# Low bits of converted weights from ScalarE into PSUM, and PSUM banks of their own for scores and for weighted sums in the first batch

## The chip, the core and the metric

The kernel runs on one core of a Trainium2 chip. A core has five engines that each take a list of instructions in order: PE (TensorE, matrix products), ACT (ScalarE), DVE (VectorE), POOL (GpSimd) and SP (SyncE, which here only issues DMAs). They work on SBUF; PE writes to PSUM, which has eight banks of 512 fp32 words in each of 128 partitions. An instruction waits on semaphores that other engines raise. The metric is device time in microseconds (us) for one execution.

## What is computed

Attention over a narrow window and over block summaries, then two mixing layers. Cut to what matters (B=4, H=8, S=768, D=64, blocks of 32, window 16, d_model 512, d_tok 256, d_ch 1536):

```python
k_sum = k.reshape(B, H, 24, 32, D).max(axis=3)
v_sum = v.reshape(B, H, 24, 32, D).mean(axis=3)
scores = concat([where(|i - j| < 16, scale * q @ k.T, -1e9), scale * q @ k_sum.T + log(32)])
a = exp(scores - max); a = a / (sum(a) + 1e-9)
x = (a @ concat([v, v_sum])).transpose -> (B, S, H * D)
h = maximum(x.T @ w_tok1, 0) @ w_tok2          # token mixing, over S
u = x + h.T
out = u + maximum(u @ w_ch1, 0) @ w_ch2        # channel mixing, over 512 -> 1536 -> 512
```

The four weights arrive as 64-bit floats, which the kernel sees as pairs of 32-bit words.

## The kernel before

**Work.** The batches are worked on one after the other. A batch has four pairs of heads; a pair has two groups of three tiles of queries. For head n and group g the names are `sc_n_g` (scores, PE, into PSUM), `e_p_g` (masked scores, DVE, then their exponentials and the row sums `den`, ACT), `et_n_g` (transposed, PE, into PSUM), `eT_n_g` (copied to SBUF, ACT) and `av_n` (weighted sum of v, PE); DVE multiplies it by `rec`, one over the row sum, into `x`. Before that DVE takes the block maxima `ks` of k, PE the block means `vm_p` of v for a pair, ACT copies them to `vs_b_p` and POOL spreads them into the rows of v that hold the summaries. Token mixing is `t1p_b_p` (PE), `t1_b_p` (its rectified high half on ACT, the low half on DVE), `up_b_half_p` (PE) and `u_b_half_p`. Channel mixing goes through the 1536 hidden columns in steps f: `hp` (24 matmuls for two steps), `h` (high half on ACT, low half on DVE) and `acc`, the sum over f.

The first batch has nothing to overlap with: its attention and token mixing run alone, and channel mixing begins when they are done. In later batches attention and token mixing are put between the steps f of the batch before.

**Conversion of weights.** Every fp32 product is made of three products of parts (high with high, high with low, low with high), so each weight is turned into two parts. `w_tick(i)` converts 512 columns of 64-bit words in SBUF. Ticks 0 to 2 make the weights of `t1p` (`wt1`), 3 to 5 those of `up` (`wt2`), and 6 to 29 in turn those of `hp` (`w1_f`) and `acc` (`w2_f`), the last of them during the first batch's channel mixing. A tick has these steps:

- ACT `absolute` (L1426): the upper word without its sign, as a float
- `clamp` (L1430): into the range of fp32, on POOL, for ticks 0 to 2 on DVE
- DVE `shift` (L1435): up three bits and masked; written to a PSUM bank `wp_i` in ticks 10 to 23, to SBUF in the others
- DVE `sign` (L1442): with the sign of the upper word
- DVE `low` (L1449): with the top three bits of the lower word
- ACT high part (L1472, twice) and POOL low part (L1478, twice), not in ticks 0 to 2

So three DVE operations are done for every tick.

**Order.** `Plan` collects every piece of work with its engine, an assumed duration, a rank and the keys that it reads and writes, plays a list schedule with assumed costs (250 GB/s for loads among them) and writes a fixed list for each engine from it. What an engine does next is never decided on the chip. Keys are pairs of a tile and a part; the framework that the lists are written in adds the semaphore waits, and it goes by tiles. Loads go through SP's list in order; eight semaphores are used in turn, so a load also waits for the eighth before it.

**Banks.** In PSUM the tag `att` has two banks, `mm` two, and `acc0` to `acc3` one each. In the first batch (`state["phase"] == "start"`) scores, transposes and weighted sums take `att, att, acc0, acc1` in turn; `vm_p` takes `acc2`, a tile for each p; `t1p` and `up` take `mm, mm, acc3` in turn. `TICKS` says after which step s of the attention how many ticks have been asked for.

Of the kernel before, what the change touches and what calls it, by code (L numbers as in the profile page):

```python
# [190 lines left out]
def tile_attention_mixer(  # L191
# [135 lines left out]

    def first_means(p):

        pt = bank(f"vm_{p}", ["acc2"])  # L330
# [5 lines left out]
        def sums():  # L336
            for t in range(NT):
                for j in range(2):
                    nc.tensor.matmul(
                        pt.t[at[j] : at[j] + NB, :D],  # L340
# [353 lines left out]
    def tok1(b, p):  # L694
        x2, a = x_t[b, p]
        pt = bank(f"t1p_{b}_{p}", ["mm", "mm", "acc3"])

        def products():
# [10 lines left out]
            writes=[(pt, 0)], rank=R_ATT,  # L709
# [1 line left out]
        split_t1(
            b, p, lambda: pt.t[:, :DTOK].rearrange("p (k c) -> p k c", k=2), (pt, 0), 0.39
# [666 lines left out]
    def w_tick(i, behind=()):  # L1379
# [31 lines left out]
        if psum:  # L1411
            pb = bank(f"wp_{i}", ["att"])
            between, bkey = (lambda: pb.t.bitcast(I32)), (pb, 0)
        else:
            between, bkey = mid, parts[0]
# [8 lines left out]
        def absolute():  # L1424
            for j, cs in enumerate(pieces):
                nc.scalar.activation(mid()[:, cs].bitcast(F32), words(j, 1).bitcast(F32), AF.Abs)  # L1426
# [19 lines left out]

        def low():
            for j, cs in enumerate(pieces):
                nc.vector.scalar_tensor_tensor(  # L1449
                    out=mid()[:, cs], in0=words(j, 0), scalar=29, in1=between()[:, cs],  # L1450
                    op0=ALU.logical_shift_right, op1=ALU.bitwise_or,
                )

        stt = 0.7 if room else 0.85
        add("act", 0.68 if room else 0.85, absolute, reads=keys, writes=parts, rank=rank)
        if first:
            add("dve", 0.45, lambda: clamp(nc.vector), writes=parts, rank=rank)
        else:
            add("pool", 0.75, lambda: clamp(nc.gpsimd), writes=parts, rank=rank)
        add("dve", 0.6 if psum else 0.5, shift, reads=parts, writes=[bkey], rank=rank)  # L1460
        add("dve", stt, sign, reads=keys, writes=[bkey], rank=rank)
        add("dve", stt, low, reads=keys + [bkey], writes=parts, rank=rank)
# [204 lines left out]
```

## Time and profile before

| | |
|---|---|
| median of 3 runs | 571.74 us (571.09 to 572.02) |
| the profiled execution | 569.56 us |
| its span in the profile | 567.6 us |
| granted TensorE clock | 1.00 throughout |
| PE, DVE, ACT, POOL busy | 552.1, 355.6, 258.2, 258.9 us |
| data moved by DMA | 99.52 MB |

The span runs from the first to the last instruction that the profiler records, so the 2.0 us between 569.56 and 567.6 lie outside it. Times inside the profile count from the span's start. An engine that is busy for 97% of the span sets the end wherever it is dense; what the others do counts only where this engine waits for them, so the places to look at are its gaps. A duration in the timeline reaches into the next instruction where the engine is pipelined; the distance between two starts is then the cost.

### The profile page before, as it was taken

Reading aid. Unit: us, or ns where it says so; the run is one execution under the profiler, and the core shown is the slowest. Engines: PE = TensorE matmul, PEld = TensorE weight load, DVE = VectorE, ACT = ScalarE, POOL = GpSimd, SP = SyncE. Lnnn points to the kernel's source line nnn. Section 1 sums busy time; section 2 is a strip of 40 time slices with the busy share of each in tenths; the row PEclk is TensorE's granted clock in tenths of the full one; section 3 lists DMA queues with packets and bytes.
Section 4 is the critical chain, followed back from the end, with each engine's and each line's share of the span. In section 5 each row is a group of like instructions: output and inputs, shape, how many; then the busy total and the mean of one; then the engine's idle time right before and its main releaser. Section 6 shows DMA issues by size and latency. Waiting matters only on the chain.

```text
span 567.6 us, 12757 instructions
## 1 busy us (share of the span) xinstructions
PE 552.1 (97%) x4629; PEld 485.3 (85%) x4629; DVE 355.6 (63%) x982; ACT 258.2 (45%) x789; POOL 258.9 (46%) x325
## 2 busy tenths in 40 slices
PE   7789999999999999999999999999999999999997
PEld 4588888868989988777799997787789999999997
DVE  4698899997474246455563335445352484899984
ACT  4677675437385334232242314242233452567642
POOL 0236586753032510157797511048879711444111
PEclk9999999999999999999999999999999999999999
DMA  8953558653656017758795606677779663643621
GB/s 267 345 169 124 193 191 274 214 179 127 203 157 194 25 39 197 189 182 208 245 261 146 139 13 189 145 189 193 192 182 313 170 263 102 203 131 97 205 92 64
DMA packets 133774, 99.52 MB, mean 175 GB/s; under 512 B 88272, under 2 KB 112464, under 8 KB 133712
## 3 DMA queue, kind: packets, MB, share of 16 engines
q1 hardware_dynamic: 133568, 98.52, 58.2%
q8 instruction: 36, 0.59, 0.4%
q14 instruction: 26, 0.21, 0.1%
q10 hardware_dynamic: 144, 0.20, 0.1%
HBM read 68.60 MB, written 28.31 MB: 171 GB/s over the span
## 4 chain that ended last, share of the span: by engine, by line
PE 76%; DVE 11%; DMA 6%; ACT 3%; issue 2%; POOL 1%; SPq 1%; ACTq 0%; DVEq 0%
PE acc L896 21%; PE hp L853 20%; PE t1q L748 5%; PE up L792 4%; PE av L558 4%; PE pb L1126 3%; PE qb L1126 3%; PE sc L427 3%; DMA w<-in_w_ch 3%; PE qa L1126 2%; PE pc L1126 2%; PE pa L1126 2%; PE qc L1126 2%; DVE wb L1449 2%; ACT e L451 1%
## 5 line engine op out<-in xcount | busy, mean ns | idle before, releaser
L896 PE MATMUL acc<-h,w 128*128 128x512 f32 (+1 forms) x864 | 165.4, 341 | 1.4 <-DVE h L870 1.4
L853 PE MATMUL hp<-u,w 128*128 128x512 f32 (+1 forms) x864 | 163.6, 339 | 0.0
L896 PEld LDWEIGHTS acc<-h,w 128*128 128x128 f32 x864 | 133.4, 189 | 21.9 <-DVE h L870 1.8
L853 PEld LDWEIGHTS hp<-u,w 128*128 128x128 f32 x864 | 133.3, 188 | 20.2 <-issue 1.3
L451 ACT ACTIVATE e<-e,den 128x120 f32<-128x120 f32 x192 | 73.3, 385 | 55.1 <-DVE den L441 39.0
L870 DVE SCALAR_TENSOR_TENSOR h<-hp,h 128x512 fp32r<-128x512 f32 (+1 forms) x72 | 39.7, 552 | 83.8 <-ACT h L865 83.6
L865 ACT ACTIVATE h<-hp 128x512 fp32r<-128x512 f32 (+1 forms) x72 | 35.1, 488 | 114.4 <-PE hp L853 113.3
L973 POOL TENSOR_TENSOR s<-s,w 128x256 f32<-128x256 f32 x84 | 61.7, 741 | 5.0
L441 DVE CUSTOM_DVE_ANT_0 e<-sc,mask_sb 128x120 f32<-128x120 f32 x192 | 41.4, 277 | 13.0 <-PE sc L427 10.8
L1478 POOL TENSOR_TENSOR w<-wb,w 128x256 fp32r<-128x256 f32 x48 | 37.7, 805 | 19.0 <-ACT w L1472 18.8
L935 POOL TENSOR_TENSOR ot<-ot,u 128x512 f32<-128x512 f32 (+1 forms) x24 | 23.8, 1019 | 43.4 <-DVE ot L927 42.6
L792 PE MATMUL up<-wt,t 128*128 128x512 f32 (+2 forms) x192 | 39.0, 343 | 0.0
L451 ACT ACTIVATION_READ_ACCUMULATOR e<-e,den 128x1 f32 x192 | 36.2, 189 | 0.0
L734 POOL TENSOR_TENSOR xs<-x,xs 128x512 fp32r<-128x512 f32 x18 | 23.6, 1310 | 25.5 <-DMA v<-vs 17.9
L410 POOL MEMSET e<- 128x48 f32 x16 | 2.2, 138 | 67.8 <-DMA away<-e 32.7
L792 PEld LDWEIGHTS up<-wt,t 128*128 128x128 f32 x192 | 30.3, 189 | 2.6
L427 PE MATMUL sc<-k,q 64*64 64x120 f32 x768 | 28.1, 271 | 1.9 <-PE et L489 0.7
L427 PEld LDWEIGHTS sc<-k,q 64*64 64x64 f32 x768 | 20.5, 132 | 10.9 <-issue 7.0
L558 PEld LDWEIGHTS av<-v,eT 120*64 120x64 f32 x768 | 24.1, 138 | 6.7 <-issue 4.5
L558 PE MATMUL av<-v,eT 120*64 120x64 f32 x768 | 26.7, 224 | 2.7 <-issue 1.1
L1472 ACT ACTIVATE w<-wb 128x256 fp32r<-128x256 f32 x48 | 18.1, 413 | 23.0 <-DVE wb L1449 22.8
L748 PE MATMUL t1q<-xs,ws 128*128 128x256 f32 x216 | 28.5, 283 | 0.0
(128 smaller groups left out, 862.1 us busy)
## 6 DMA issues: line engine op xcount, KB each, us to landing
w<-in_w_ch SPq DMA_DIRECT2D x48, 256.0 KB
k<-in_kw SPq DMA_DIRECT2D x16, 720.0 KB
v<-in_vw SPq DMA_DIRECT2D x32, 288.0 KB
q<-in_q SPq DMA_DIRECT2D x16, 384.0 KB
away<-e SPq DMA_DIRECT2D x16, 384.0 KB
eT<-away SPq DMA_DIRECT2D x64, 96.0 KB
sums<-s SPq DMA_DIRECT2D x24, 256.0 KB
w2d<-w SPq DMA_DIRECT2D x12, 512.0 KB
```

The costliest lines, as they stand in the source:

```text
L427: nc.tensor.matmul(tiles[j].t[c * QT : (c + 1) * QT, i * NC : (i + 1) * NC], lhsT=qt.t[rows, t * QT : (t + 1) * QT], rhs=kt.t[rows, t, :], ...
L441: nc.vector.tensor_tensor_reduce(out=e.t[:, j, i * P : i * P + NC], in0=tiles[j].t[:, i * NC : (i + 1) * NC], in1=mask_sb[:, mv, :], op0=A ...
L451: nc.scalar.activation(ei, ei, AF.Exp, bias=den_t[n].t[:, 1, T : T + 1], scale=-1.0, accum_out=den_t[n].t[:, 0, T : T + 1],)
L558: nc.tensor.matmul(pv[cs, T], lhsT=eT[:NC, T % (TT // 2), cs], rhs=v.t[:NC, 2 * T + c], start=True, stop=True,)
L748: nc.tensor.matmul(pt.t[:, 2 * P * k : 2 * P * (k + 1)], lhsT=ws[:, wp, T, ks], rhs=xs[:, xp, T], start=(c == 0 and k == 0 and T == 0 and ...
L792: nc.tensor.matmul(pt.t[:, :nt], lhsT=t1.t[:, part, ks], rhs=wt2[w].t[:, k, h0 : h0 + nt], start=(far and k == 0 and i == 0), stop=(k == D ...
L853: nc.tensor.matmul(pt.t[:, :nt], lhsT=w1_t[f].t[:, w, c], rhs=us[c].t[:, part], start=(i == 0), stop=(i == len(ops) - 1),)
L870: lambda: nc.vector.scalar_tensor_tensor(out=h.t[:, 1], in0=pt.t[:, :nt], scalar=0.0, in1=h.t[:, 0].bitcast(F32), op0=ALU.max, op1=ALU.sub ...
L896: nc.tensor.matmul(slot.t[:, c0 : c0 + nt], lhsT=w2_t[f].t[:, w, o * P : (o + 1) * P], rhs=h.t[:, part], start=(f == 0 and w == 0 and part ...
L973: nc.gpsimd.tensor_tensor(out=out_, in0=left, in1=right, op=op)
L1126: nc.tensor.matmul(bank_.t[:, :HS], lhsT=w(i), rhs=x(j), start=first and n == 0, stop=True, skip_group_check=True,)
L1478: lambda hi=hi, lo=lo, source=source: nc.gpsimd.tensor_tensor(out=lo(), in0=source(), in1=hi().bitcast(F32), op=ALU.subtract),
```

## The change

**Conversion.** `absolute` now scales the upper word by 2^-80, with the clamp's bounds scaled alike. A new ACT step `last_bits` reads the lower word as an unsigned integer and writes its top three bits as an integer into a PSUM bank. `shift` becomes one DVE operation that shifts the clamped word and ors it with these bits, in PSUM; `sign` ands the result with the upper word's sign and writes it to SBUF. `low` is gone. The clamp is on POOL for all ticks. All 30 ticks use a PSUM bank: `acc3` for ticks 0 to 5, `acc0` and `acc1` in turn for 6 to 9, `att` from 10 on. Ticks 3 to 5 get the rank of attention, and tick 6 is asked for later (the entry `12: 7` is gone).

**Banks of the first batch.** Scores alone rotate over `att, att, acc0, acc1`. Transposes and weighted sums take `mm, mm`. All `vm_p` and all `t1p` share one tile, `vm_bank` on `acc2`: `t1p` its first 256 columns, `vm_p` 64 columns each behind them. `up` of the first two pairs take `acc3`, of the last two `acc0, acc1, att, att`.

**Plan.** Loads before 25 us are costed at 360 GB/s.

```diff
-    RATE, LAND = 250.0, 2.2
+    RATE, FIRST, LAND = 250.0, 360.0, 2.2
...
         "start": ["att", "att", "acc0", "acc1"],
+        "turned": ["mm", "mm"],
...
+    def att_bank(name, turned=False):
+        start = state["phase"] == "start"
+        return bank(name, BANKS["turned" if turned and start else state["phase"]])
+
+    def tok_bank(name, late):
+        if state["phase"] == "start":
+            return bank(name, ["acc0", "acc1", "att", "att"] if late else ["acc3"])
         return bank(name, BANKS[state["phase"]])
...
+    vm_bank = plan.slot(ps, [P, 512], F32, "acc2", "vm", 1)
...
-        pt = bank(f"vm_{p}", ["acc2"])
+        pt, cs = vm_bank, slice(DTOK + D * p, DTOK + D * (p + 1))
...
-            pt = att_bank(f"et_{n}_{g}")
+            pt = att_bank(f"et_{n}_{g}", True)
...
-            pt, v, den = att_bank(f"av_{n}"), v_t[n], den_t[n]
+            pt, v, den = att_bank(f"av_{n}", True), v_t[n], den_t[n]
...
-        pt = bank(f"t1p_{b}_{p}", ["mm", "mm", "acc3"])
+        pt = vm_bank
...
-        first, rank = two[0][2] is None, R_ATT if i < TOKT else R_W
-        psum = 10 <= i < 24
+        first, rank = two[0][2] is None, R_ATT if i < 6 else R_W
...
+        pb = bank(f"wp_{i}", ["acc3"] if i < 6 else ["acc0", "acc1"] if i < 10 else ["att"])
+        bits = lambda: pb.t.bitcast(I32)
...
+        def last_bits():
+            for j, cs in enumerate(pieces):
+                nc.scalar.activation(
+                    bits()[:, cs], words(j, 0).bitcast(U32), AF.Copy, bias=LOW_BIAS,
+                    scale=LOW_SCALE,
+                )
...
         def shift():
-            nc.vector.tensor_scalar(
-                out=between(), in0=mid(), scalar1=3, scalar2=0x3FFFFFFF,
-                op0=ALU.logical_shift_left, op1=ALU.bitwise_and,
+            nc.vector.scalar_tensor_tensor(
+                out=bits(), in0=mid(), scalar=3, in1=bits(),
+                op0=ALU.logical_shift_left, op1=ALU.bitwise_or,
             )
 
         def sign():
             for j, cs in enumerate(pieces):
                 nc.vector.scalar_tensor_tensor(
-                    out=between()[:, cs], in0=words(j, 1), scalar=-0x40000000,
-                    in1=between()[:, cs], op0=ALU.bitwise_and, op1=ALU.bitwise_or,
+                    out=mid()[:, cs], in0=words(j, 1), scalar=0x7FFFFFFF, in1=bits()[:, cs],
+                    op0=ALU.bitwise_or, op1=ALU.bitwise_and,
                 )
 
-        def low():
-            for j, cs in enumerate(pieces):
-                nc.vector.scalar_tensor_tensor(
-                    out=mid()[:, cs], in0=words(j, 0), scalar=29, in1=between()[:, cs],
-                    op0=ALU.logical_shift_right, op1=ALU.bitwise_or,
-                )
...
-    TICKS = {3: 3, 8: 6, 12: 7, 17: 9, 19: 10}
+    TICKS = {3: 3, 8: 6, 17: 9, 19: 10}
```

The lists come out of the plan anew. Three places of them matter below. On SP, among the first batch's loads, the token weights of tick 2 were followed by these before (the number behind a name is that of its buffer):

```order
L269 DMA v_4_338<-in_vw 96x768
L269 DMA v_5_357<-in_vw 96x768
L269 DMA k_3_364<-in_kw 128x1440
L269 DMA q_3_366<-in_q 128x768
L1396 DMA w_3_368<-in_w_tok2 128x512 x2
```

In the changed kernel k_3 and q_3 come first at the same place:

```order
L280 DMA k_3_282<-in_kw 128x1440
L280 DMA q_3_284<-in_q 128x768
L280 DMA v_4_364<-in_vw 96x768
L280 DMA v_5_384<-in_vw 96x768
L1406 DMA w_3_387<-in_w_tok2 128x512 x2
```

So v of the third pair of heads has moved behind k and q of the fourth; the two blocks have the same bytes together.

On ACT, in the first batch, this stood before around the copy `t1_0_1` of the second `t1p` (L682) and the copy `vs_0_3` of the last block means (L359; e_2_1 is finished ahead of the piece):

```order
L682 ACTIVATE t1_0_1_629<-t1p_0_1_584 128x256
L1472 ACTIVATE wt2_0_632<-wb_3_573 128x256 x2
L451 ACTIVATE e_3_0_638,den_6_639<-e_3_0_638,den_6_639 128x120
L500 ACTIVATE eT_4_1_654<-et_4_1_634 120x384
L500 ACTIVATE eT_5_1_659<-et_5_1_642 120x384
```

In the changed kernel the same part of ACT's list reads (L695 is the copy `t1`, L372 `vs`, L1432 `absolute`, L1438 `last_bits`, L1477 the high part, L464 the exponential):

```order
L695 ACTIVATE t1_0_0_668<-vm_200 128x256
L1438 ACTIVATE wp_4_670<-w_4_435 128x512
L464 ACTIVATE e_2_1_532,den_4_398<-e_2_1_532,den_4_398 128x120
L372 ACTIVATE vs_0_3_688<-vm_200 24x64 x2
L1432 ACTIVATE wb_5_693<-w_5_474 128x512
L464 ACTIVATE e_2_1_532,den_5_405<-e_2_1_532,den_5_405 128x120
L1477 ACTIVATE wt2_0_637<-wb_4_628 128x256 x2
L1438 ACTIVATE wp_5_700<-w_5_474 128x512
L695 ACTIVATE t1_0_1_703<-vm_200 128x256
L464 ACTIVATE e_2_1_532,den_4_398<-e_2_1_532,den_4_398 128x120
L464 ACTIVATE e_2_1_532,den_5_405<-e_2_1_532,den_5_405 128x120
L464 ACTIVATE e_3_0_574,den_6_575<-e_3_0_574,den_6_575 128x120
```

`vs_0_3`, which stood behind eT_5_1 and the first two exponentials of e_3_1, has moved ahead of four exponentials of e_2_1, and the tile that it reads, `vm`, is also the one that `t1p` is written to.

On PE, behind the block means of the last pair, the changed kernel has (the first row is t1p_0_1):

```order
L714 MATMUL vm_200<-x_0_0_362,wt1_367 128x128 x12
L502 MATMUL et_4_1_710<-identf_66,e_2_1_532 120x128 x3
L502 MATMUL et_5_1_716<-identf_66,e_2_1_532 120x128 x3
L571 MATMUL av_4_731<-v_4_364,eT_4_0_609 64x64 x6
L571 MATMUL av_4_731<-v_4_364,eT_4_1_721 64x64 x6
L571 MATMUL av_5_746<-v_5_384,eT_5_0_625 64x64 x6
L571 MATMUL av_5_746<-v_5_384,eT_5_1_729 64x64 x6
L502 MATMUL et_6_0_772<-identf_66,e_3_0_574 120x128 x3
L502 MATMUL et_7_0_777<-identf_66,e_3_0_574 120x128 x3
```

Before, t1p_0_1 stood ahead of the scores of the last pair and those ahead of et_4_1; the block means of the last pair came only behind av_5 and the pair's second scores. Now they stand ahead of t1p_0_1, and et_4_1 follows it at once.

More of the change, by code (lines that the diff above doesn't have):

```diff
@@ L14 @@
 I32 = mybir.dt.int32
+U32 = mybir.dt.uint32
 AF = mybir.ActivationFunctionType
@@ L41 @@
 HALF = NF // 2
-HI_MAX = 122879.9921875
+HI_SCALE = 2.0**-80
+HI_MIN, HI_MAX = 2.0**-95, 122879.9921875 * HI_SCALE
+LOW_SCALE = 2.0**-29 * (1 - 2.0**-20)
+LOW_BIAS = 7.5 * 2.0**-20 - 0.5
 NU = B * H
@@ L151, in _order @@
                 if w.kb:
-                    dma = max(dma, now) + w.kb / self.RATE
+                    dma = max(dma, now) + w.kb / (self.RATE if now > 25 else self.FIRST)
                     w.end = dma + self.LAND
@@ L351, in first_means @@
         add(
-            "pe", 1.6, sums, reads=[(v_t[2 * p], 0), (v_t[2 * p + 1], 0)], writes=[(pt, 0)],
+            "pe", 1.6, sums, reads=[(v_t[2 * p], 0), (v_t[2 * p + 1], 0)], writes=[(pt, p)],
             rank=R_H,
@@ L359, in first_means @@
                 lambda j=j: nc.scalar.activation(
-                    s.t[WIN:NC, j * D : (j + 1) * D], pt.t[at[j] : at[j] + NB, :D], AF.Copy
+                    s.t[WIN:NC, j * D : (j + 1) * D], pt.t[at[j] : at[j] + NB, cs], AF.Copy
                 ),
-                reads=[(pt, 0)], writes=[(s, j)], rank=R_EVAC,
+                reads=[(pt, p)], writes=[(s, j)], rank=R_EVAC,
             )
@@ L708, in tok1 @@
             "pe", 2.8, products, reads=x_keys(b, p) + [(wt1, i) for i in range(3)],
[L709 removed]
+            writes=[(pt, "t")], rank=R_ATT,
         )
         split_t1(
[L712 removed]
+            b, p, lambda: pt.t[:, :DTOK].rearrange("p (k c) -> p k c", k=2), (pt, "t"), 0.39
         )
@@ L769, in tok2 @@
         h0, nt = H0[b][half], HT[b][half]
-        pt = bank(
-            f"up_{b}_{half}_{p}",
-            ["mm", "mm", "acc3"] if state["phase"] == "start" else BANKS[state["phase"]],
-        )
+        pt = tok_bank(f"up_{b}_{half}_{p}", p >= NP - 2)
         tag, bufs, whole = f"u{half}", 4, b == B - 1
@@ L1410, in w_tick @@
             mid = lambda: wb.t
[L1411 to L1415, printed above, removed]
+        pb = bank(f"wp_{i}", ["acc3"] if i < 6 else ["acc0", "acc1"] if i < 10 else ["att"])
+        bits = lambda: pb.t.bitcast(I32)
         n = 512 if room else 256
@@ L1442, in sign @@
                 nc.vector.scalar_tensor_tensor(
-                    out=between()[:, cs], in0=words(j, 1), scalar=-0x40000000,
-                    in1=between()[:, cs], op0=ALU.bitwise_and, op1=ALU.bitwise_or,
-                )
-        def low():
-            for j, cs in enumerate(pieces):
-                nc.vector.scalar_tensor_tensor(
-                    out=mid()[:, cs], in0=words(j, 0), scalar=29, in1=between()[:, cs],
-                    op0=ALU.logical_shift_right, op1=ALU.bitwise_or,
[L1452 to L1462, printed above, removed]
+                    out=mid()[:, cs], in0=words(j, 1), scalar=0x7FFFFFFF, in1=bits()[:, cs],
+                    op0=ALU.bitwise_or, op1=ALU.bitwise_and,
+                )
+        spent = 0.66 if room else 0.85
+        add("act", spent, absolute, reads=keys, writes=parts, rank=rank)
+        add("pool", 0.75, clamp, writes=parts, rank=rank)
+        add("act", spent, last_bits, reads=keys, writes=[(pb, 0)], rank=rank)
+        add("dve", 0.7, shift, reads=parts, writes=[(pb, 0)], rank=rank)
+        add("dve", 0.7 if room else 0.85, sign, reads=[*keys, (pb, 0)], writes=parts, rank=rank)
         for j in range(0 if first else 2):
@@ L1516, in tile_attention_mixer @@
                 tok2(0, 0, p - 1)
-    while tick < 10:
+    while tick < TICKS[19]:
         w_tick(tick)
```

13 lines of the change are left out of this document (7 added, 6 removed).

## The prediction

> **What bounds the kernel now.** I read the page first, for the engine that ends the span.
>
> ```profile
> PE 552.1 (97%) x4629; PEld 485.3 (85%) x4629; DVE 355.6 (63%) x982; ACT 258.2 (45%) x789; POOL 258.9 (46%) x325
> PE 76%; DVE 11%; DMA 6%; ACT 3%; issue 2%; POOL 1%; SPq 1%; ACTq 0%; DVEq 0%
> ```
>
> PE is busy 97% of the span and carries 76% of the chain that ended last, so a conversion that costs VectorE less is worth only what PE now waits for. The windows view says where PE waits (start:end, length, then busy time and count of PE, PEld, DVE, ACT, POOL, the granted clock, the DMA share, GB/s).
>
> ```profile
> 8.00:29.70 21.70, 16.32 (x357) 12.49 (x349) 14.57 (x69) 14.98 (x63) 3.19 (x4) 1.00 1.01 323
> 29.70:65.50 35.80, 33.35 (x435) 30.31 (x433) 32.08 (x105) 26.95 (x93) 18.22 (x24) 1.00 0.45 144
> 65.50:115.90 50.40, 50.40 (x218) 40.64 (x217) 46.75 (x79) 29.59 (x70) 37.66 (x54) 1.00 0.71 227
> 115.90:118.00 2.10, 0.70 (x4) 0.25 (x2) 2.10 (x6) 1.01 (x3) 1.29 (x3) 1.00 0.61 240
> 118.00:160.00 42.00, 41.65 (x445) 35.63 (x445) 30.32 (x111) 20.42 (x82) 10.78 (x12) 1.00 0.48 156
> 160.00:540.00 380.00, 378.96 (x3020) 340.24 (x3021) 210.33 (x583) 154.00 (x460) 182.19 (x220) 1.00 0.60 170
> 540.00:567.60 27.60, 23.89 (x134) 22.96 (x133) 17.54 (x31) 9.97 (x19) 4.86 (x4) 1.00 0.21 75
> ```
>
> PE's idle time by row is 5.4 us, 2.4, 0, 1.4, 0.35, 1.0 and 3.7. The stretch to 65.5 is the first batch's attention and token mixing, and at 65.53 the first channel-mixing matmul (`hp`) starts. From there the work is the same in both kernels and PE is dense apart from one hole. So only two things count: **when the first `hp` starts**, and **the 1.40 us hole** at 116. PE's timeline has both (start, duration, line, tiles, count, idle time before and its releaser):
>
> ```profile
> 28.23 1.53 PE L339 MATMUL vm<-v,means 96*24 96x64 f32 x48
> 29.69 2.94 PE L701 MATMUL t1p<-x,wt 128*128 128x128 f32 x24
> 35.59 0.92 PE L489 MATMUL et<-identf,e 128*120 128x128 f32 x6 [1.40 <-ACT e L451]
> 41.26 1.62 PE L558 MATMUL av<-v,eT 120*64 120x64 f32 x48 [0.50 <-DVE den L441]
> 50.23 1.27 PE L558 MATMUL av<-v,eT 120*64 120x64 f32 x36 [0.48 <-ACT eT L500]
> 65.53 5.75 PE L853 MATMUL hp<-u,w 128*128 128x512 f32 x24
> 117.94 2.60 PE L896 MATMUL acc<-h,w 128*128 128x512 f32 x10 [1.40 <-DVE h L870]
> ```
>
> 1.40 + 0.50 + 0.48 is the whole 2.4 us of idle time between 29.7 and 65.5.
>
> **The hole at 116.** PE waits for the low half of `h`, which VectorE made late:
>
> ```profile
> 117.21 0.68 DVE L870 SCALAR_TENSOR_TENSOR h<-hp,h 128x512 fp32r<-128x512 f32 x1
> 111.84 4.08 POOL L1478 TENSOR_TENSOR w<-wb,w 128x256 fp32r<-128x256 f32 x4
> L1449 DVE SCALAR_TENSOR_TENSOR wb<-w,wb 128x512 int32<-128x512 int32 x2 | 2.2, 1114 | 0.1
> L1449 DVE SCALAR_TENSOR_TENSOR wb<-w,wp 128x512 int32<-128x512 int32 x10 | 6.9, 686 | 0.3
> ```
>
> VectorE is full there (2.10 of 2.10), and 46.75 of 50.40 in the stretch before. With both inputs in SBUF (`w,wb`) an operation took 1114 ns beside GpSimd's; with one in PSUM (`w,wp`) 686. The change leaves two operations a tick, each with one input in PSUM: 2 x 0.69 = 1.38 us, where three are at least 2.06 and up to 3.3 by these rows. Two ticks and one `h` split (0.68) are 3.4 us of VectorE for one f, that is for 24 matmuls, which take 5.75 of PE. I take all of the hole as gone: **-1.4 us**, bounds 0 and -1.75 (with the next row's 0.35).
>
> The price is ScalarE's new `last_bits`, 512 columns into PSUM, which no row shows. Nearest are a plain 512-column pass and one that reads PSUM:
>
> ```profile
> L1426 ACT ACTIVATE wb<-w 128x512 f32<-128x512 f32 x6 | 3.9, 679 | 0.9 <-POOL w L1478 0.9
> L831 ACT ACTIVATE u<-up 128x512 fp32r<-128x512 f32 x4 | 2.4, 590 | 2.2 <-PE up L792 2.2
> ```
>
> I take 0.57, an `abs` with the overlap of its successor off (bounds 0.48 to 0.68). Some 18 ticks between 65.5 and 116 add 18 x 0.57 = 10 us to ScalarE's 29.6 of 50.4: room, if its order is right.
>
> **The start of the batch.** k_3 and q_3 are now loaded ahead of v_4 and v_5, and PE is handed vm of pair 2 (which needs v_5) ahead of the et_2_1 and et_3_1 transposes. When v_5 lands is read from the bytes.
>
> ```profile
> 0.00:4.00 4.00, 2.81 (x7) 1.04 (x8) 0.65 (x3) 1.28 (x1) 0.77 (x7) 1.00 0.51 176
> 4.00:8.00 4.00, 4.00 (x27) 1.73 (x29) 1.26 (x2) 0.00 (x0) 0.00 (x0) 1.00 1.01 356
> 8.00:16.00 8.00, 5.93 (x128) 4.54 (x120) 5.50 (x42) 7.09 (x35) 0.00 (x0) 1.00 1.04 279
> 16.00:24.00 8.00, 6.12 (x150) 5.08 (x150) 3.65 (x17) 4.47 (x18) 3.19 (x4) 1.00 1.00 341
> 24.00:26.70 2.70, 1.80 (x14) 0.89 (x8) 2.56 (x6) 2.70 (x12) 0.00 (x0) 1.00 0.91 356
> 5.06 0.95 DVE L312 TENSOR_REDUCE ks<-k 128x24 f32<-128x768 f32 x1 [3.28 <-DMA k<-in_kw]
> ```
>
> By 26.7 these rows moved 704 + 1424 + 2232 + 2728 + 961 = 8049 KB; four k (737 each), four q (393), the mask (184), six v (295) and six pieces of token weight (262) are 8048. The queues are full all along, so the order inside them doesn't move the last one. k_0's 737 KB were through at 4.1 and VectorE began on it at 5.06, a lag of 0.95, so v_5 is in SBUF at 27.65 and vm of pair 2 runs to 29.1 (1.46 a piece, 28.23 to 29.69), 0.6 earlier than now. The two transposes come behind it instead of ahead: 0.87. Left for PE are 33.35 + 0.87 = 34.2 us before the first `hp`. ks_1 on VectorE now stands ahead of the first exponentials (0.95) and is covered by the wait for v_5; without that cover it would cost the 0.95. In ticks 0 to 2 the clamp goes from VectorE to GpSimd, which has 3.19 of 21.70 us busy there, and `last_bits` to ScalarE; tick 2 is done by about 29, and t1p_0_0, which needs it, starts at 34.
>
> By the Trainium skill (DMA: Bandwidth & Descriptors, Measured) one core's HBM loads are bounded by about 358 GB/s, or higher with its neighbour idle. Here 4 to 8 us and 24 to 26.7 us agree with 356, but 8 to 16 us moved 279.
>
> **The shared bank.** All vm of pairs 0 to 3 and all four t1p now lie in one tile and bank, and it orders what had tiles of its own. The program's semaphores say who waits: t1_0_0 on ScalarE for the end of *vm of pair 3*, which PE runs right behind t1p_0_0; t1p_0_1 on PE for VectorE's low half of t1_0_0; vs_0_3 on ScalarE, which only needs vm of pair 3, for the end of *t1p_0_1*. ScalarE takes its list in order, so abs of tick 5, three e_2_1, hi of tick 4, last_bits of tick 5, t1_0_1 and all of e_3_0 stand behind vs_0_3, and PE's et_4_1 and et_5_1, next after t1p_0_1, need the last e_2_1. Durations:
>
> ```profile
> L451 ACT ACTIVATE e<-e,den 128x120 f32<-128x120 f32 x48 | 18.3, 385 | 10.5 <-DVE den L441 10.4
> 31.26 0.46 ACT L359 ACTIVATE vs<-vm 24x64 f32<-24x64 f32 x2
> 36.53 0.85 ACT L500 ACTIVATE eT<-et 120x384 f32<-120x384 f32 x2
> 39.22 0.38 ACT L682 ACTIVATE t<-t1p 128x256 fp32r<-128x256 f32 x1 [0.53 <-PE t1p L701]
> 39.50 0.71 ACT L1472 ACTIVATE wt<-wb 128x256 fp32r<-128x256 f32 x2
> 39.64 0.42 DVE L687 SCALAR_TENSOR_TENSOR t<-t1p,t 128x256 fp32r<-128x256 f32 x1 [0.40 <-ACT t L682]
> 39.12 0.85 PE L427 MATMUL sc<-k,q 64*64 64x120 f32 x24
> 56.96 2.84 PE L701 MATMUL t1p<-x,wt 128*128 128x128 f32 x24
> 59.64 0.38 PE L784 MATMUL up<-identf,x 128*128 128x128 f32 x2
> 60.57 0.38 PE L784 MATMUL up<-identf,x 128*128 128x128 f32 x2
> 61.51 0.60 PE L784 MATMUL up<-identf,x 128*128 128x128 f32 x4
> 63.34 0.42 PE L784 MATMUL up<-identf,x 128*128 128x128 f32 x2
> ```
>
> A pitch is taken from start to start where rows follow each other: t1p 2.7 (56.96 to 59.64), up of 256 columns 0.93, of 512 1.83; a row by itself loses the 0.05 to 0.1 by which it overlaps the next. From 29.1 PE runs et (0.87), sc (0.8), av of two heads (1.55), sc (0.8), et (0.87), t1p_0_0 (2.7) and vm (1.46) to 38.1, none of it late: ScalarE's vs, two eT and six e for et_4_0 (0.46 + 0.76 + 2.28) are done by 32.7. ScalarE then does t1_0_0, last_bits and one e and is at vs_0_3 by 39.4. Four waits follow:
> - t1p ended at 39.12 and VectorE had its low half at 40.06, so the way back costs 0.95: t1p_0_1 runs from 39.1 to 41.8. **1.0.**
> - vs_0_3 starts at 41.9, 2.5 after ScalarE came to it. To the last e_2_1: vs 0.46, abs 0.57, e 0.38, hi 0.61, last_bits 0.57, t1 0.28, two e 0.76, together 3.6; et_5_1 ends at 45.9, after 0.87 of work. **3.2.**
> - Two e_3_0 (0.76) stand ahead of eT_4_1, so av_4 starts at 46.8. **0.9.**
> - hi of tick 5 and four e_3_0 (0.61 + 1.5) end at 49.2, et_7_0 at 49.4, where av_5 ended at 48.4. **0.2.**
>
> Past that ScalarE is ahead of PE. From 49.4 four up of 512 columns (7.3), four of 256 (3.7), two t1p (5.4), et (0.87) and av (1.55) make 18.9, and the first `hp` starts at 68.3. Two of these up now share banks with the conversion of ticks 8 and 9 and wait for its end; by ScalarE's list that is some 2.5 us before PE comes to them, and w1_0 of tick 6, moved 5 steps back, has some 10 us. The total the other way round, 29.1 + 34.2 + 5.3 = 68.6, agrees; I take 68.4. Against 65.53 that is **+2.9**; bounds +1.9 (a third of the waits taken up) and +3.9 (a second missed turn on ScalarE).
>
> By the Trainium skill (PSUM — Partial Sum Buffer, PSUM bank collisions raise a hardware error) PSUM is to be guarded by bank and quadrant, not by address, so disjoint columns of a bank don't free two engines of each other. No run here shows a collision; the waits in the program fit the rule.
>
> **Sum.** +2.9 - 1.4 = **+1.5 us**. The profiled execution took 569.56 (567.6 of span and 2.0 around it), so 571.1 by it; the runs shown have a median of 571.74, 2.2 above it, and it is against these that I forecast: **573.2**.
>
> **Rivals.**
> - *The bank's waits cost nothing*: ScalarE reaches vs_0_3 only when t1p_0_1 has ended anyway, and the first `hp` starts at 29.1 + 34.2 + a wait like today's 2.0 to 2.4, about 65.3. For it: 26.95 of 35.80 us of ScalarE are busy there now, and new work makes it later. Against: it is there 2.5 us before. -0.2 to -0.6, and -1.4: **569.9**, faster.
> - *The hole moves to ScalarE*: `last_bits` stands ahead of an `h` pass in its fixed order, and PE waits there as it did for VectorE. It decides where ScalarE comes to `h` over 2 us late, which 40 of 50 busy doesn't ask for. +2.9 + 0: **574.6**.
> - *The loads run faster*: at 356 GB/s throughout, the best two rows, 8049 KB would be through at 22.6 and vm of pair 2 doesn't wait for v_5; PE gains the 0.9 us that it idles in the last of the rows on the loads (2.70 - 1.80). 573.2 - 0.9: **572.3**, no change. Against it: the bytes and the queues are those of before.
>
> **How the numbers follow.** This kernel's measurement can tell some 0.2%, 1.14 us, from no change: faster is under 570.6, slower over 572.9. The forecast has 0.60 (0.43 slower, 0.16 same, 0.01 faster by the bounds of its two terms), the free bank 0.17 (0.14 faster, 0.03 same), the hole on ScalarE 0.13 (slower), the faster loads 0.10 (0.08 same, 0.02 slower). Together: faster 0.15, same 0.27, slower 0.58. With +1.9 - 1.75 and +3.9 - 0.6 as ends and the free bank's upper part inside, the range is 570.2 to 575.2.
>
> **What would show it.** Right: the first `hp` at 67.5 to 69.5; an idle time of about 3 us ahead of `et` near 45, released by ScalarE's `e`; vs_0_3 starting at the end of t1p_0_1 with ScalarE idle for over 2 us before it; no hole over 0.4 us between the first `hp` and 160. Wrong: the first `hp` before 66 (the bank is free), PE idle ahead of `acc` behind an `h` of ScalarE (the hole moved), vm of pair 2 starting before 27 (the loads), or vm of pair 3 waiting for its v, which I take to be there.

## The result, and the profile after

| | before | after |
|---|---|---|
| median of the runs taken together | 571.41 us (568.20 to 572.02, 4 runs) | 578.76 us (578.08 to 579.62, 4 runs) |
| ratio, with its 95% interval | 1 | 1.0138 (1.0111 to 1.0164) |
| the profiled execution, its span | 569.56, 567.6 us | 578.08, 576.0 us |
| first `hp` starts | 65.53 us | 75.57 us |
| from there to the end of the span | 502.07 us | 500.43 us |
| mean granted TensorE clock of the profiled execution | 1.00 | 0.982 |

The changed kernel is 1.4% slower: 5.6 us above the forecast of 573.2 and outside its range. The first batch became 10.0 us longer, the rest 1.6 us shorter. From the page of the changed kernel, the busy times, the granted clock in 40 slices of 14.4 us, and the chain by engine:

```profile
PE 559.1 (97%) x4629; PEld 493.2 (86%) x4629; DVE 330.6 (57%) x941; ACT 274.4 (48%) x827; POOL 256.3 (44%) x328
PEclk9886999999999999999999999999999999999999
PE 90%; DMA 6%; SPq 1%; issue 1%; ACT 1%; DVE 0%; DVEq 0%
```

PE makes the same 4629 matmuls and is busy 7.0 us longer with them. That can't come from waits, which make PE idle and not busy. The second row says where it comes from: in slices 2 to 4, from 14 to 58 us, PE wasn't granted its full clock. VectorE lost 25 us of work and ScalarE gained 16. The windows view puts the stages beside those shown for the kernel before (columns as there):

```profile
8.00:29.70 21.70, 15.27 (x319) 12.70 (x320) 14.97 (x81) 16.33 (x64) 5.04 (x7) 0.84 1.04 319
29.70:75.50 45.80, 40.51 (x480) 36.85 (x477) 23.69 (x80) 33.17 (x109) 18.61 (x27) 0.85 0.42 132
75.50:126.00 50.50, 50.50 (x219) 40.72 (x219) 38.33 (x66) 39.83 (x97) 38.05 (x57) 1.00 0.70 222
126.00:168.00 42.00, 42.00 (x467) 35.74 (x466) 25.53 (x116) 22.61 (x87) 9.38 (x10) 1.00 0.57 169
168.00:548.00 380.00, 379.72 (x3000) 341.24 (x2999) 208.03 (x567) 150.71 (x453) 179.58 (x218) 1.00 0.59 168
548.00:576.00 28.00, 24.29 (x138) 23.38 (x136) 18.12 (x32) 10.44 (x20) 4.85 (x4) 0.99 0.23 80
```

From the first `hp` on PE is dense; the hole is gone, and with it some smaller ones. The loss is all in the first two rows, which have more idle time (6.4 and 5.3 us, where before it was 5.4 and 2.4) and a clock of 0.84 and 0.85. PE's timeline has both kinds of loss side by side (`vm` from L714 is `t1p`, which lives in the shared tile):

```profile
11.71 0.92 PE L440 MATMUL sc<-k,q 64*64 64x120 f32 x24 [2.30 <-DVE k L332]
13.29 2.76 PE L352 MATMUL vm<-v,means 96*24 96x64 f32 x46 [0.32 <-DMA v<-in_vw]
28.08 0.29 PE L352 MATMUL vm<-v,means 96*24 96x64 f32 x2 [2.85 <-DMA v<-in_vw]
29.32 2.70 PE L352 MATMUL vm<-v,means 96*24 96x64 f32 x46 [0.95 <-DMA v<-in_vw]
31.95 1.28 PE L502 MATMUL et<-identf,e 128*120 128x128 f32 x6
36.97 2.84 PE L714 MATMUL vm<-x,wt 128*128 128x128 f32 x24
40.54 1.52 PE L352 MATMUL vm<-v,means 96*24 96x64 f32 x46 [0.50 <-DMA v<-in_vw]
42.99 4.57 PE L714 MATMUL vm<-x,wt 128*128 128x128 f32 x24 [0.93 <-DVE t L700]
47.40 0.38 PE L502 MATMUL et<-identf,e 128*120 128x128 f32 x2
51.15 1.11 PE L502 MATMUL et<-identf,e 128*120 128x128 f32 x4 [3.36 <-ACT e L464]
52.74 2.83 PE L571 MATMUL av<-v,eT 120*64 120x64 f32 x48 [0.49 <-ACT eT L513]
55.51 1.49 PE L502 MATMUL et<-identf,e 128*120 128x128 f32 x6
75.57 5.75 PE L863 MATMUL hp<-u,w 128*128 128x512 f32 x24
```

Compare equal work. Two t1p of 24 matmuls take 2.84 us at 36.97 and 4.57 at 42.99; the means of a pair take 1.52 at 40.54, but 2.76 at 13.29 and 2.70 at 29.32; the weighted sums that took 1.62 before take 2.83 at 52.74. Each slow one stands right behind idle time. The windows view of those four places has the granted clock in its third column from the right (the last row is the whole stretch around 52.74):

```profile
12.40:19.20 6.80, 6.48 (x88) 5.24 (x81) 3.75 (x27) 4.82 (x23) 1.59 (x2) 0.50 1.02 330
29.30:32.00 2.70, 2.68 (x47) 2.50 (x47) 2.60 (x15) 0.00 (x0) 0.00 (x0) 0.52 0.88 301
43.00:47.50 4.50, 4.50 (x25) 4.50 (x26) 1.38 (x2) 0.40 (x2) 0.00 (x0) 0.62 0.04 14
52.20:55.50 3.30, 2.81 (x49) 2.67 (x48) 0.91 (x4) 3.30 (x16) 1.41 (x2) 0.50 0.06 11
49.90:56.70 6.80, 5.07 (x57) 4.34 (x58) 3.23 (x9) 6.19 (x27) 3.40 (x5) 0.50 0.13 42
```

So the waits that the prediction counted were there, and behind them PE ran at about half its clock, which the prediction didn't count. That is one theory: **idle time costs twice, once as a wait and once as a low clock behind it**. A second is that the low clock is only a companion and the whole loss is in the waits and the loads. The experiments are to tell these apart and to price the parts of the change.

### The profile page after: what moved, and what is told of

It reads as the page before. It is cut to its first block, busy times and chain, and to the rows that moved or that the text cites. A ratio compares the mean times of both kernels' runs of the same rounds, so it can differ in the third digit from the quotient of the medians.

```text
span 576.0 us, 12780 instructions
## 1 busy us (share of the span) xinstructions
PE 559.1 (97%) x4629; PEld 493.2 (86%) x4629; DVE 330.6 (57%) x941; ACT 274.4 (48%) x827; POOL 256.3 (44%) x328
## 4 chain that ended last, share of the span: by engine, by line
PE 90%; DMA 6%; SPq 1%; issue 1%; ACT 1%; DVE 0%; DVEq 0%
PE hp L863 26%; PE acc L906 26%; PE up L802 6%; PE t1q L761 5%; PE av L571 4%; DMA v<-in_vw 4%; PE sc L440 3%; PE pb L1136 3%; PE qb L1136 3%; PE qa L1136 2%; PE pc L1136 2%; PE pa L1136 2%; PE qc L1136 2%; PE et L502 2%; PE vm L352 1%; DMA away<-e 1%
## 5 line engine op out<-in xcount | busy, mean ns | idle before, releaser
L863 PE MATMUL hp<-u,w 128*128 128x512 f32 (+1 forms) x864 | 165.4, 341 | 0.0
L464 ACT ACTIVATE e<-e,den 128x120 f32<-128x120 f32 x192 | 73.3, 384 | 54.8 <-DVE den L454 42.8
L1483 POOL TENSOR_TENSOR w<-wb,w 128x256 fp32r<-128x256 f32 x48 | 34.5, 741 | 11.5 <-ACT w L1477 11.5
L464 ACT ACTIVATION_READ_ACCUMULATOR e<-e,den 128x1 f32 x192 | 36.2, 189 | 0.0
L584 DVE TENSOR_TENSOR x<-av,rec 128x384 f32<-128x384 f32 x32 | 17.5, 553 | 19.4 <-PE av L571 18.4
```

Of the source, the lines that this page charges most:

```text
L464: nc.scalar.activation(ei, ei, AF.Exp, bias=den_t[n].t[:, 1, T : T + 1], scale=-1.0, accum_out=den_t[n].t[:, 0, T : T + 1],)
L863: nc.tensor.matmul(pt.t[:, :nt], lhsT=w1_t[f].t[:, w, c], rhs=us[c].t[:, part], start=(i == 0), stop=(i == len(ops) - 1),)
```

## The experiments

Each kernel ran beside the kernel before on the same chip; ratios are to that one. "Clock" is the range of the mean granted clock over a kernel's executions, from its results. The kernel before has medians from 570.33 to 571.41 us on these chips, so differences between the medians of two kernels are good to about 1 us. The last column is of one execution only, and that can be a lucky one: kernel 1's is the fastest of its ten.

| kernel | median us | ratio (95%) | clock | first `hp`, profiled |
|---|---|---|---|---|
| after | 578.76 | 1.0138 (1.0111 to 1.0164) | 0.982 to 0.985 | 75.57 |
| 1: vm of pair 3 on another bank | 573.14 | 1.0037 (1.0013 to 1.0060) | 0.987 to 0.994 | 66.19 |
| 2: early filler matmuls | 579.05 | 1.0150 (1.0108 to 1.0192) | 0.985 to 0.988 | 76.21 |
| 3: 1 and 2 | 573.39 | 1.0044 (1.0022 to 1.0067) | 0.988 to 0.994 | 69.44 |
| 4: before, with the new conversion only | 567.43 | 0.9945 (0.9918 to 0.9972) | 0.993 to 0.997 | 65.73 |
| 5: 1, and v loaded first | 570.65 | 0.9975 (0.9941 to 1.0009) | 0.987 to 0.999 | 67.03 |
| 6: long fillers | 579.37 | 1.0131 (1.0090 to 1.0171) | 0.994 to 1.00 | 76.07 |
| 7: the plan told of the shared tile | 575.70 | 1.0073 (1.0047 to 1.0100) | 0.984 to 0.991 | 71.72 |
| 8: short fillers | 574.57 | 1.0076 (1.0048 to 1.0104) | 0.999 to 1.00 | 70.30 |
| 9: 4, with short fillers | 567.00 | 0.9937 (0.9918 to 0.9956) | 0.998 to 1.00 | 65.61 |
| 10: 5, with short fillers | 567.18 | 0.9942 (0.9921 to 0.9963) | 0.999 to 1.00 | 63.58 |

**1. The shared tile.** The means of pair 3 alone get a bank of their own; PE and ScalarE keep the order of their lists.

```diff
     def first_means(p):
         pt, cs = vm_bank, slice(DTOK + D * p, DTOK + D * (p + 1))
+        if p == NP - 1:
+            pt = bank("vm_3", ["att"])
```

> The changed kernel, with vm of pair 3 alone in a bank of tag att; the lists of PE and ScalarE keep their order, only the waits through the shared tile go. If the bank makes the waits and the waits make the clock fall (theory): no idle time of 0.9 ahead of t1p_0_1 and none of 3 ahead of et_4_1, vs_0_3 starts right behind vm of pair 3, the clock stays at 1.00 from 33 us on, and the first hp comes 8 to 9 us earlier than in the changed kernel (near 67): 570 to 571. If the clock falls for another reason (rival): only the 4.8 us of idle time go, t1p_0_1 still takes 4.4 us, about 574. If the bank is not the cause (second rival): no change, 578.8.

The time fell by 5.6 us against after, to 573.14. PE's timeline of this kernel, at the places of the three waits:

```profile
39.41 2.94 PE L716 MATMUL vm<-x,wt 128*128 128x128 f32 x24
43.21 0.70 PE L504 MATMUL et<-identf,e 128*120 128x128 f32 x4 [0.63 <-ACT e L466]
44.80 1.62 PE L573 MATMUL av<-v,eT 120*64 120x64 f32 x48 [0.90 <-ACT eT L515]
```

t1p_0_1 doesn't wait (it starts where the means end), `et` waits 0.63 instead of 3.36, and behind these short idle times PE runs at full speed: 2.94 and 1.62 us where after had 4.57 and 2.83. The mechanism is the one expected; the median isn't, since this execution took 569.35 us and the median is 573.14, where 570 to 571 was expected. So the shared tile is the largest single cause among those tested, waits and slow stretches together. What is left against before is smaller than 1% and needs another cause.

**2 and 3. Is the early low clock the reason that v comes late?** In after, v_4 is issued only when `av` of the first pair has freed its buffer. Nine matmuls into a bank that nobody reads keep PE's clock up ahead of the second pair's scores, so that `av` is earlier; 3 has edit 1 as well.

```diff
         def products():
+            for _ in range(9 if (p, g) == (1, 0) else 0):
+                nc.tensor.matmul(pw.t, lhsT=warm.t[:, :P], rhs=warm.t, start=True, stop=True)
```

> The changed kernel with nine more matmuls on the zeroed warm tile ahead of the scores of pair 1, where PE idles for 2.30 us behind ks_1. If that idle time lowers the clock from 12 to 19 us, makes av_0 late and so the load of v_4 (theory): the clock stays at 1.00 to 25 us, av_0 ends near 19.5 in place of 22.0, v_4 is issued before 20.5 in place of 22.25, vm of pair 2 waits under 1.5 us in place of 3.8 and runs at full clock; the first hp comes 3 to 4 us earlier: about 575. The waits near 43 and 51 stay. If the low clock there is hidden by the load (rival): within 0.5 us of 578.8.

> Both edits of the two kernels before. If the two causes are separate and together all of it (theory): the gains add up to 11 to 12 us, the first hp near 64.5, the hole at 116 of the kernel before is gone, clock 1.00: 567 to 569, faster than before. If one hides the other (rival): no faster than the better of the two, 570 to 571.

The theory that the early low clock makes v late fell. Its first half held: the early scores wait 0.74 us instead of 2.30, and v_4 is issued at 19.75 instead of 22.25. PE's timeline of kernel 2 shows that this didn't help:

```profile
27.53 0.29 PE L352 MATMUL vm<-v,means 96*24 96x64 f32 x2 [4.80 <-DMA v<-in_vw]
28.66 2.75 PE L352 MATMUL vm<-v,means 96*24 96x64 f32 x46 [0.84 <-DMA v<-in_vw]
```

PE came to the means earlier and waited longer, 4.80 us instead of 2.85, for a v that was issued 2.5 us earlier and came only 0.66 earlier than in after (28.66 against 29.32). Work saved ahead of a load that is late anyway turns into idle time, here even into the kind that is followed by a slow stretch (2.75 us for the means). Kernel 3 is level with 1, where 567 to 569 was expected.

**4. The conversion alone.** The kernel before, with `last_bits` and two VectorE operations in ticks 10 to 29 only, and none of the new banks, loads or ranks.

```diff
+        if i < 10:
...
+        else:
+            add("act", spent, new_absolute, reads=keys, writes=parts, rank=rank)
+            add("pool", 0.75, new_clamp, writes=parts, rank=rank)
+            add("act", spent, last_bits, reads=keys, writes=[bkey], rank=rank)
+            add("dve", 0.7, new_shift, reads=parts, writes=[bkey], rank=rank)
+            add("dve", 0.7 if room else 0.85, new_sign, reads=[*keys, bkey], writes=parts, rank=rank)
```

> The kernel before with the new conversion in ticks 10 to 29 alone; banks, loads and the first batch's lists up to the first hp as before. If the conversion is worth the hole (theory): the first hp at 65.5 as before, no idle time of PE near 116, 1.4 us faster than before: 570.0. If ScalarE's new work is late for h (rival): holes ahead of acc, no change or slower, 571.4 to 573.

It is faster than before by 0.55% (0.28 to 0.82%), and 11.3 us faster than after. The first `hp` stays where it was (65.73), and from there to the end it takes 499.17 us, 2.9 less than before and twice the 1.4 that was expected. So the conversion does what it is for, and **the whole loss lies in what the first batch got with it**. Its profile also shows that a low clock doesn't need a long wait. PE's timeline, then the windows view up to the fall of the clock and behind it:

```profile
22.36 1.09 PE L432 MATMUL sc<-k,q 64*64 64x120 f32 x24 [0.73 <-PE et L494]
24.48 0.54 PE L494 MATMUL et<-identf,e 128*120 128x128 f32 x3 [0.43 <-ACT e L456]
28.12 2.76 PE L344 MATMUL vm<-v,means 96*24 96x64 f32 x48
```

```profile
21.60:25.00 3.40, 2.23 (x30) 1.40 (x29) 2.82 (x14) 3.40 (x14) 0.00 (x0) 1.00 0.89 266
25.10:31.90 6.80, 6.24 (x78) 5.16 (x79) 6.56 (x24) 2.92 (x12) 0.64 (x1) 0.50 0.85 300
```

In the 3.4 us ahead of the fall PE is idle for 1.17 us in all, with no single idle time over 0.73. The kernel before has nearly the same there, and its profiled execution kept the full clock. Its timeline and windows:

```profile
23.08 1.09 PE L427 MATMUL sc<-k,q 64*64 64x120 f32 x24 [0.73 <-PE et L489]
25.20 0.54 PE L489 MATMUL et<-identf,e 128*120 128x128 f32 x3 [0.43 <-ACT e L451]
22.70:26.10 3.40, 2.21 (x29) 1.40 (x29) 2.82 (x11) 3.40 (x14) 0.00 (x0) 1.00 0.92 311
24.00:29.70 5.70, 4.27 (x85) 2.88 (x79) 5.42 (x11) 3.41 (x13) 0.00 (x0) 1.00 0.97 358
```

So behind idle times as short as these the clock may fall in one execution and not in another.

**5. The order of the loads.** Edit 1, and k_3 and q_3 are loaded behind v_4 and v_5, as before the change (the cut shows k; q has the same). The plan then gives parts of PE's list in another order too.

```diff
-        return load(k_t[p], lambda t: t, kw[b, hp], 737)
+        return load(k_t[p], lambda t: t, kw[b, hp], 737, behind=[state["v"]] if p == 3 else ())
```

> The kernel of e1_vm3_att with k_3 and q_3 loaded behind v_4 and v_5, as before the change; the plan then orders parts of the first batch anew. If the late v is what is left of the loss (theory): v_5 is there by 25.5, vm of pair 2 waits under 1 us (2.2 in e1's profile, 6 in e3's), no stretch of low clock from 25 to 33, the first hp near 64, 568 to 570. If the wait only moves to the scores of pair 3, which then wait for k_3 (rival): 572 to 574, as e1.

A further 2.5 us, to 570.65, a little over the 568 to 570 expected. The means of pair 2 start 4.2 us earlier than in after. From PE's timeline of kernel 5:

```profile
24.00 0.29 PE L354 MATMUL vm<-v,means 96*24 96x64 f32 x2 [1.06 <-DMA v<-in_vw]
25.13 2.75 PE L354 MATMUL vm<-v,means 96*24 96x64 f32 x46 [0.84 <-DMA v<-in_vw]
```

SyncE issues the two v at 19.97 in this kernel and at 22.25 in after, where k_3 (19.01) stands ahead. The early issue alone isn't what counts: kernel 2 issued them as early, at 19.75, but behind k_3 (16.44) and q_3 (18.20), and its means came at 28.66 all the same. So the place among the loads moves the transfer that PE waits for by some 3.5 us, though the bytes are the same. The slow stretch behind the wait is still there (2.75).

**6 and 8. Is the low clock a cause or a companion?** The changed kernel, all its banks, loads and waits kept, with products of the identity ahead of the places where PE waits; they write columns that the next matmul overwrites. In 6 they are 44, 10 and 22; in 8 they are 24, 3 and 10, with the nine of kernel 2.

```diff
         def sums():
+            for _ in range({2: 24, 3: 3}.get(p, 0)):
+                nc.tensor.matmul(
+                    pt.t[:, cs], lhsT=identf, rhs=identf[:, :D], start=True, stop=True
+                )
...
-            def flip(j=j, pt=pt):
+            def flip(j=j, pt=pt, n=n):
+                for _ in range(10 if (n, g) == (4, 1) else 0):
+                    nc.tensor.matmul(
+                        pt.t[:, :P], lhsT=identf, rhs=identf, start=True, stop=True
+                    )
```

> The changed kernel with matmuls of the identity ahead of three waiting pieces of PE: 44 of 64 columns ahead of vm of pair 2, 10 ahead of vm of pair 3, 22 of 128 columns ahead of et_4_1, written where the real ones write afterwards. The waits for data stay as they are. If the fall of the clock behind the idle times is part of the loss (theory): clock 1.00 from 29 to 57, t1p_0_1 takes 2.7 us in place of 4.4, av_4 and av_5 1.6 in place of 2.8, the first hp near 70.5 in place of 75.6: 573 to 575. If the low clock is hidden by waits (rival): within 1.5 us of 578.8.

> e6 with fillers that end ahead of the data: nine matmuls on the warm tile ahead of the scores of pair 1, 24 of the identity (0.23 us each, as e6 showed) ahead of vm of pair 2, 3 ahead of vm of pair 3, 10 ahead of et_4_1. If the low clock costs on top of the waits (theory): clock near 1.00 from 12 to 57, vm of pair 2 at 29 in 1.5 us, t1p_0_1 2.7 us, the first hp at 70 to 71: 573 to 575, 4 to 6 less than the changed kernel. By the slope over the 20 runs of before in the first job (0.35 us for each 0.001 of mean clock) going from 0.985 to 1.0 is worth 5 us. If the low clock is hidden by the waits (rival): 577 or more.

Kernel 6 (579.37 us, level with after, at a clock of 0.994 to 1.00) decides nothing. Its PE timeline shows the 44 fillers ahead of the means of pair 2 (an fp32 product is two records) and those means:

```profile
22.36 10.04 PE L351 MATMUL vm<-identf 128*128 128x64 f32 x88
32.34 1.53 PE L356 MATMUL vm<-v,means 96*24 96x64 f32 x48
```

The fillers cost 10.04 / 44 = 0.23 us each, so they ran 3 us past the time (29.32) at which v had come in after, and put back as much as the clock gave; the 22 ahead of et_4_1 took 5.08 us, where the wait was 3.36. In kernel 8 they end about when v is there. PE's timeline of kernel 8, at the places shown for after:

```profile
28.85 1.53 PE L356 MATMUL vm<-v,means 96*24 96x64 f32 x48
40.77 2.94 PE L724 MATMUL vm<-x,wt 128*128 128x128 f32 x24 [0.94 <-DVE t L710]
47.30 0.70 PE L512 MATMUL et<-identf,e 128*120 128x128 f32 x4 [1.13 <-ACT e L470]
48.90 1.62 PE L581 MATMUL av<-v,eT 120*64 120x64 f32 x48 [0.90 <-ACT eT L523]
70.30 5.75 PE L873 MATMUL hp<-u,w 128*128 128x512 f32 x24
```

The waits are as they were (0.94; 1.13 behind 2.40 of fillers, together 3.5), and the work behind them takes 1.53, 2.94 and 1.62 us instead of 2.70, 4.57 and 2.83. The median falls from 579.0 (after and kernel 2 are level) to 574.6. The nine early fillers by themselves (kernel 2) had given nothing. So **the low clock is a cause of its own, and costs the changed kernel some 4 us**: 4.4 by the medians, 3.5 by the ratios of after and kernel 8 to the kernel before, whose intervals don't touch. It may be somewhat more, since PE reaches the means only at 28.85 here, by its fillers and not by v.

**7. A plan that knows of the shared tile.** `vm_p` and `t1p` get one key in place of keys by part, so that the list schedule sees the waits that the framework adds.

```diff
-            "pe", 1.6, sums, reads=[(v_t[2 * p], 0), (v_t[2 * p + 1], 0)], writes=[(pt, p)],
+            "pe", 1.6, sums, reads=[(v_t[2 * p], 0), (v_t[2 * p + 1], 0)], writes=[(pt, 0)],
```

> The changed kernel with one key for the whole shared tile, so that the plan orders by the waits that the tile really makes. If the loss comes from an order made without those waits (theory): ScalarE no longer stands over 2 us at a vs, and the time is that of e1 or better, 570 to 573. If one tile for vm and t1p is too little whatever the order (rival): 575 or more.

575.7: better than after by 3 us, worse than a second bank by 2.6. Waits of 4.18 us (for q) and 2.31 (for v, on GpSimd) took the place of those removed. Knowing the conflict isn't enough here: in the one order that the plan found with it, one tile for both still costs more than two.

**9 and 10. Nothing left?** Kernel 4 with 17 short fillers between 9 and 27 us, and kernel 5 with the nine of kernel 2 and nine products of the identity ahead of the means of pair 2.

```diff
+    def keep_busy(times):
+        for _ in range(times):
+            nc.tensor.matmul(pw.t, lhsT=warm.t[:, :P], rhs=warm.t, start=True, stop=True)
```

> The kernel of e4_conversion with 17 short matmuls on the warm tile ahead of pieces of PE that wait between 9 and 27 us. If low clock in some executions is what spreads e4's and the kernel before's times (theory): mean clock 0.998 or more in most runs, 565.5 to 566.5, up to 1.5 us faster than e4's 567.4. If the fillers end later than the data (rival): as e4 or slower, 567.5 to 569.

> The kernel of e5_v_first with nine matmuls on the warm tile ahead of the scores of pair 1 and nine of the identity ahead of vm of pair 2, so with all three causes taken away: no wait through the shared tile, v before k, no low clock. If these are the whole loss (theory): mean clock 0.998 or more, 565 to 567, level with e9 (567.0), which has the old banks; e5's one run at clock 0.999 had a span of 564.0. If the new banks cost something besides (rival): 568 or more.

Kernel 9 is level with 4: 0.4 us can't be told from nothing, and the 565.5 to 566.5 expected wasn't reached. Kernel 10, which keeps the new conversion, the new banks but one and the early v, comes to 567.18, level with 4 and 9, and starts the first `hp` at 63.58, 2.0 us ahead of the kernel before. So the loss of the changed kernel is accounted for: 579.0 to 567.2 is 11.8 us, of which 4.4 are the low clock (kernel 8) and 7.4 the shared tile and the order of the loads, with the lists that the plan wrote for them (8 to 10; no run parts these at full clock).

## Why the prediction was wrong, step by step

The first batch by its steps: the time of each in us, in the forecast, in kernel 8 (full clock) and in after.

| step | forecast | kernel 8 | after |
|---|---|---|---|
| vm of pair 2 ends | 29.1 | 30.30 | 31.95 |
| t1p_0_1 starts | 39.1 | 40.77 | 42.99 |
| av_4 starts | 46.8 | 48.90 | 52.74 |
| et_7_0 ends | 49.4 | 51.55 | 56.83 |
| first `hp` | 68.4 | 70.30 | 75.57 |

- **The shared bank: right.** vs_0_3 started where t1p_0_1 ended, as said, with ScalarE idle for 4.25 us ahead of it (2.5 forecast; t1p_0_1 was the slow one, and in kernel 8, at full clock, it is 2.63). The exponentials of e_2_1 that stand behind vs_0_3 are three, as the list ahead of the prediction and its working have it, not the four that the sentence below that list says. ScalarE's timeline of after, around it:

```profile
42.92 0.38 ACT L464 ACTIVATE e<-e,den 128x120 f32<-128x120 f32 x1
47.65 0.46 ACT L372 ACTIVATE vs<-vm 24x64 f32<-24x64 f32 x2 [4.25 <-issue]
48.13 0.68 ACT L1432 ACTIVATE wb<-w 128x512 f32<-128x512 f32 x1
```

The three waits were forecast at 1.0, 3.2 and 0.9 us and came at 0.93, 3.36 and 0.49; the fourth, of 0.2, didn't show.
- **The conversion: right.** Groups of after, by form, between 76 and 130 us (count, then busy us and mean ns, then idle before):

```profile
L1450 DVE SCALAR_TENSOR_TENSOR wp<-wb,wp 128x512 int32<-128x512 int32 x19 | 13.1, 690 | 3.2 <-POOL wb L1445 1.9 <-ACT wp L1438 1.1
L1457 DVE SCALAR_TENSOR_TENSOR wb<-w,wp 128x512 int32<-128x512 int32 x14 | 9.6, 683 | 0.3
L1438 ACT ACTIVATE wp<-w 128x512 int32<-128x512 uint32 x13 | 8.0, 624 | 0.0
```

690 + 683 is 1.37 us a tick on VectorE (1.38 forecast). `last_bits` takes 624 ns by itself and some 0.56 from start to start (0.57 forecast), and ScalarE's 39.83 us of 50.5 is the 29.6 + 10 of the prediction. The hole went, and no other came: -1.64 against -1.4. The other kernels with the same list behind the first `hp` have between -1.8 and 0 there, by single waits further on.
- **The loads: a step that failed.** "The queues are full all along, so the order inside them doesn't move the last one" put v_5 in SBUF at 27.65. PE began on it at 29.32 in after, at 28.66 in kernel 2 and at 25.13 in kernel 5, with the same bytes. The sum of the bytes came out: after moved 306 GB/s over its first 26.4 us, which is 8.08 MB, where the working had 8.05 by 26.7.

```profile
0.00:26.40 26.40, 21.42 (x327) 14.77 (x327) 13.71 (x78) 14.80 (x54) 5.75 (x14) 0.87 0.95 306
```

But the sum doesn't say which transfer the bytes belong to. The token weights that SyncE issues from 23.32 on, behind v, ran beside it: from 25 to 28 us about half the bytes moved in packets of 3072 bytes, the size of v's and q's, and half in those of 2048, the size of the weights'. From 25.2 to 28.0 the queues moved 232 GB/s in all, where the last row of the working had 356. In kernel 8 the means end 1.2 us late; ahead of those of pair 3, whose v was taken to be there, it has 0.71 us of fillers where after waited 0.50. The two, less 0.3 us won between them, are nearly the whole 1.7 us that kernel 8 is late at t1p_0_1.
- **The clock: the step that failed most.** The sum worked out the idle times of PE and priced the work behind them by rows of before, all at 1.00, so the low clock was a term of nothing. Between kernel 8 and after, where the fillers are the difference, the first `hp` moves by 5.3 us, and the medians by 4.4. None of the rivals had it. That the kernel would get slower, and by the bank's waits, was right; the 1.5 us of the sum came out as 7.4.
- **The median.** The 2.2 us between before's profiled execution and its median were carried over as a constant. They go with a low clock as well: of 61 executions of the kernel before, beside the experiments, the six at 0.999 or more have a median of 569.7 us, the 17 at 0.991 or less one of 572.7. The profiled one was of the first kind. So a clock of 1.00 in one profile was no property of the kernel.

From a forecast of 571.1 at full clock, kernel 8 stands 3.5 us higher: 1.9 of it at the first `hp`, 0.9 behind it (501.6 us to the end, where 500.7 were forecast), 0.7 outside the span and between its profiled execution and its median. The low clock adds 4.4 to that, and the 2.2 already in the forecast for the median are to be taken off: 573.2 - 2.2 + 3.5 + 4.4 = 578.9. The range took 0.6 off at its upper end for the hole, whose own bound was 0; with 0 it would have ended at 575.6, still below what was measured.

Behind the first `hp`, after needs 500.4 us and kernels 1, 5, 8 and 10 need 501.4 to 502.1. PE runs the same list of matmuls there in all of these, by their names in the traces, and the single waits that the timeline shows make up the differences: 0.28 us in after, 0.92 in kernel 1, 0.23 and 1.03 in 5, 0.49 and 0.48 in 8, 1.87 in 10. Without them all five need 500.2 to 500.6. What stays open is the rest: kernels 4 and 9, with the old banks, need 498.9 without their waits of 0.32 and 0.88. Their list differs in 24 of 3816 places, and no run here shows what makes the 1.5 us.

## What to carry to other kernels

Where PE is the bound and a stage has idle times of half a microsecond and more, reckon that an idle time can cost twice: as a wait, and as work behind it at half speed until the clock is back; and look at the granted clock of several executions, since one profile at 1.00 may be the lucky one. Two pieces of work that share a tile wait for each other by the whole tile, whatever columns they use, and on engines that take their lists in order the wait is paid by everything behind it: look for the instruction that only needs the *other* piece. And before costing a load by its bytes, find the transfer that is waited for and its place in the queue.

## What the hardware showed that was not expected

In after PE's granted clock fell to half four times, for 3.4 or 6.8 us, at idle time. It was 0.50 from 12.4 to 19.2 us (behind 2.30 us idle), from 29.4 to 32.8 (behind 2.85 and 0.95), from 43.1 to 46.5 (behind 0.50 and 0.93) and from 49.9 to 56.7 (within and behind 3.36). The Trainium skill (TensorE: Matmul & The Clock Gate, Part 1: The HAM clock gate) has half the clock as the gate's only other setting, in windows of about 3.4 us that run freely, so that one kernel differs from execution to execution. The half (0.50), the lengths (3.4 and 6.8 us) and the differences (means of 0.984 to 1.00 over the 61 executions of the kernel before) agree with it. The Trainium skill (the same page, Why this matters for your kernels) advises against idle gaps over some 3 us. Here less was enough: in kernel 4 the clock fell behind single gaps of 0.73 and 0.43 us, with 1.17 of 3.4 us idle, though the same gaps left it at 1.00 in the profiled execution of the kernel before. Short filler matmuls in such gaps, 17 to 46 of them, kept 0.998 to 1.00 in all executions of kernels 8, 9 and 10. A low clock doesn't always cost: kernel 4 had it from 25.1 to 31.9 us, and lost nothing that could be measured against kernel 9.
